# First input block on one DMA queue, the second block held back, the first block's scaling moved ahead, and one idle matmul dropped

## The chip, the cores and the metric

The kernel runs on one core of one Trainium2 chip. The metric is the device time of one execution in microseconds (us); "span" is the profiler's stretch from the first to the last instruction of the program, which is about 1.8 us shorter. Some executions on this chip are slower as a whole. Ratios are computed as the mean time of one kernel's fast runs over the mean of the other's in the same rounds, so they are not quite the ratio of the medians that are quoted beside them.

A timeline line reads: start and duration in us, engine, source line, operation, tile written<-tile read, sizes, count; in brackets the engine's idle time before it and what ended that. PE is TensorE's matmuls, PEld its weight loads, DVE VectorE, ACT ScalarE, POOL GpSimd; SPq and ACTq are DMA issues by SyncE and ScalarE.

## The reference

Four residual layers on x of 2048 rows by 1024 columns in bf16: linear attention, gated MLP, and both again with the same weights.

```python
x = A_x
x = x + _A_ref(_layernorm(x), A_wqkv, A_wo)          # q, k, v = x @ wqkv; linear attention; @ wo
x = x + _B_ref(_layernorm(x), B_W_gate, B_W_up, B_W_down)
x = x + _A_ref(_layernorm(x), A_wqkv, A_wo)
x = x + _B_ref(_layernorm(x), B_W_gate, B_W_up, B_W_down)
```

## The kernel before

x is cut into 16 blocks of 128 rows. The first attention layer normalises block by block, transposes (blocks 0 and 1 on TensorE, later ones by DMA) and projects. A unit is eight matmuls of one block against one weight tile of 1 MB; K has tiles k0 and k1, Q has q0 and q1. The order of the first units is k0 of blocks 0 and 1, k1 of blocks 0 and 1, q0 of blocks 0 and 1, then k0, k1, q0 of block 2 and of block 3, then q1.

```python
def head(self):
    ...
    for _ in range(11):                                  # idle matmuls on zeros
        nc.tensor.matmul(idle, lhsT=zero[:, 0:P], rhs=zero, start=True, stop=True)
    k0, k1, v0, q0, q1 = (ring.place() for _ in range(5))
    self.load_x(0, 0)                                    # SyncE's queue
    self.load_x(0, 1, nc.scalar)                         # ScalarE's queue
    k0(0, H)
    self.load_x(1, None, nc.scalar)
    k0(H, 2 * H)
    self.load_x(2)
    k1()
    self.load_x(3)
    def load():                                          # called in the fourth unit
        for t in range(4, 8):
            self.load_x(t)
        q1()
        ...

def block0():
    stat(0, 0); stat(0, 1); rstd(0)
    stat(1, 0)                                           # block 1's first statistic
    scale(0, 0); scale(0, 1)
    t0 = turn(0, 0); t1 = turn(0, 1)                     # TensorE transposes
    t0("ss")
    stat(1, 1); rstd(1)
    q0(0, 2 * H, self.nc.scalar)                         # q0 on ScalarE's queue
    t1("v")
    k(0, 0, between)          # between(): block 1's scaling and first transposes,
                              # ahead of the last two of the eight matmuls
```

## Time and profile before

| | before |
|---|---|
| time, median of the first 3 runs | 1627.14 us |
| span of the profiled run | 1625.4 us |
| TensorE busy | 1613.2 us, 99% |
| VectorE busy, whole span | 567.7 us, 35% |

TensorE is busy practically all the time, so what counts is when its unbroken work starts and whether it is ever interrupted.

### The profile page before, as it was taken

The page shows a single profiled execution, that of the slowest core. Times are in us where ns is not written, and L with a number is a line of the kernel's source. Part 1 is how long each engine was busy: PE and PEld are TensorE (multiplying, and loading weights), DVE is VectorE, ACT ScalarE, POOL GpSimd, SP SyncE. Part 2 cuts the span into 40 slices and gives each one's busy share as a digit, 9 for nine tenths or more (in the row PEclk, how much of TensorE's full clock was granted, in tenths as well). Part 3 has the DMA queues.
Part 4 walks back from the last instruction along what each step waited for, and adds up shares of the span by engine and source line. Part 5 has one row for each costly group of instructions (what it writes and reads, how often), then busy time and mean ns, then how long its engine had stood idle before and what let it go on. Part 6 is the DMA issues. An engine that isn't in the chain of part 4 may idle for free.

```text
span 1625.4 us, 18607 instructions
## 1 busy us (share of the span) xinstructions
PE 1613.2 (99%) x7605; PEld 739.4 (45%) x7739; DVE 567.7 (35%) x940; ACT 330.4 (20%) x635; POOL 202.1 (12%) x134
## 2 busy tenths in 40 slices
PE   9999999999999999999999999999999999999999
PEld 4444444444444444444444444444444444444444
DVE  8844694113212222222264447932021112111211
ACT  6741212101110210111067312121011101101110
POOL 1449220000000000000023582100000000000000
PEclk9999999999999999999999999999999999999999
DMA  9314547447455545544550157464654455454442
GB/s 269 55 52 66 172 79 203 146 158 215 156 162 195 156 147 165 160 154 139 166 111 1 54 107 240 86 189 145 193 161 152 154 178 155 146 170 150 155 162 71
DMA packets 300358, 235.58 MB, mean 145 GB/s; under 512 B 103408, under 2 KB 296304, under 8 KB 300272
## 3 DMA queue, kind: packets, MB, share of 16 engines
q1 hardware_dynamic: 294192, 228.75, 48.3%
q10 hardware_dynamic: 6080, 5.64, 1.0%
q8 instruction: 60, 0.98, 0.3%
q14 instruction: 26, 0.21, 0.0%
HBM read 201.33 MB, written 8.39 MB: 129 GB/s over the span
## 4 chain that ended last, share of the span: by engine, by line
PE 99%; issue 0%; DMA 0%; DVE 0%; ACT 0%
PE pu L643 24%; PE pg L643 24%; PE acc L667 23%; PE ps L410 14%; PE ps L536 7%; PE ps L445 7%; PE kv L458 0%; PE acc_last L667 0%; DMA x<-in_A_x_dram 0%; PE fold L521 0%; PE tp L262 0%; PE ps L435 0%; ACT L692 0%; DVE xo L684 0%; DVE x L156 0%
## 5 line engine op out<-in xcount | busy, mean ns | idle before, releaser
L643 PEld LDWEIGHTS <-t 128*128 128x128 bf16 x3584 | 350.7, 98 | 422.8
L643 PE MATMUL pu<-xnT,t 128*128 128x512 bf16 x1756 | 420.1, 379 | 2.0
L643 PE MATMUL pg<-xnT,t 128*128 128x512 bf16 x1756 | 419.8, 379 | 1.8
L667 PE MATMUL acc<-t,hT 128*128 128x512 bf16 x1728 | 380.6, 379 | 1.9
L649 DVE TENSOR_TENSOR hT<-pu,rg 128x512 bf16<-128x512 f32 x224 | 154.8, 691 | 571.5 <-PE pu L643 555.0
L648 ACT ACTIVATE rg<-pg 128x512 f32<-128x512 f32 x224 | 133.5, 596 | 736.1 <-PE pg L643 661.7
L667 PEld LDWEIGHTS <-hT 128*128 128x128 bf16 x1820 | 178.1, 98 | 209.0
L410 PE MATMUL ps<-t,xnT 128*128 128x512 bf16 x1024 | 223.4, 379 | 0.2 <-ACT xnT L272 0.2
L410 PEld LDWEIGHTS <-xnT 128*128 128x128 bf16 x1024 | 99.4, 98 | 120.0 <-issue 1.5
L536 PE MATMUL ps<-T,pqT 128*128 128x512 bf16 x500 | 110.2, 379 | 0.6
L147 ACT ACTIVATE rstd<-mv,eps 128x1 f32<-128x1 f32 x64 | 18.8, 294 | 337.7 <-DVE mv L145 337.5
L684 DVE TENSOR_TENSOR xo<-x,acc 128x512 bf16<-128x512 f32 x31 | 21.3, 687 | 170.3 <-PE acc L667 169.5
L489 POOL TENSOR_TENSOR prod<-pq,zrow 128x1024 f32<-128x1024 bf16 x32 | 68.0, 2125 | 85.9 <-DVE den L494 72.4
L140 DVE BATCH_NORM_STATS2 stats<-x 128x6 f32<-128x512 f32 (+1 forms) x120 | 77.9, 671 | 1.2 <-DMA x<-in_A_x_dram 0.4
L536 PEld LDWEIGHTS <-pqT 128*128 128x128 bf16 x512 | 49.9, 98 | 60.4 <-issue 0.5
L425 POOL CAST ksum<-x 128x512 f32<-128x512 bf16 x2 | 1.7, 866 | 605.4 <-DVE x L361 605.4
L681 DVE TENSOR_TENSOR x<-x,acc 128x512 f32<-128x512 f32 x32 | 21.6, 674 | 138.5 <-PE acc L667 137.4
L427 POOL TENSOR_TENSOR ksum<-ksum,slab 128x512 f32<-128x512 f32 x46 | 54.1, 1183 | 80.3 <-DVE slab L361 63.0
L361 DVE SCALAR_TENSOR_TENSOR pq<-ps,e 128x512 bf16<-128x512 f32 x64 | 43.9, 686 | 53.3 <-ACT e L355 51.3
L501 POOL TENSOR_TENSOR pq<-pq,den 128x1024 bf16<-128x1024 bf16 x32 | 61.7, 1936 | 3.1 <-DVE den L496 3.1
L494 DVE TENSOR_REDUCE den<-prod 128x32 f32<-128x1024 f32 x32 | 38.9, 1217 | 54.0 <-POOL prod L489 54.0
L445 PE MATMUL ps<-slab,x 128*128 128x512 bf16 x249 | 55.7, 379 | 0.4
(57 smaller groups left out, 592.5 us busy)
## 6 DMA issues: line engine op xcount, KB each, us to landing
t<-in_B_W_gate_dram SPq DMA_DIRECT2D x56, 1024.0 KB, 7.3
t<-in_B_W_up_dram SPq DMA_DIRECT2D x56, 1024.0 KB, 5.4
t<-in_B_W_down_dram SPq DMA_DIRECT2D x64, 896.0 KB, 5.1
t<-in_A_wqkv_dram SPq DMA_DIRECT2D x10, 1024.0 KB, 5.1
t<-in_A_wo_dram SPq DMA_DIRECT2D x4, 1024.0 KB, 6.7
away<-x SPq DMA_DIRECT2D x8, 512.0 KB, 4.7
x<-away SPq DMA_DIRECT2D x8, 512.0 KB, 8.2
out_dram<-xo ACTq DMA_DIRECT2D x31, 128.0 KB, 2.5
```

What stands on the lines that cost most here:

```text
L140: self.nc.vector.bn_stats(out=stats[:, c, :], in_=src[:, c * fmax:(c + 1) * fmax])
L361: nc.vector.scalar_tensor_tensor(out=out, in0=ps, scalar=0.0, in1=e, op0=ALU.max, op1=ALU.add)
L410: nc.tensor.matmul(by_row(ps), lhsT=self.xnT[l, l_q][:, kt, j * P:(j + 1) * P], rhs=w[:, kt, :].rearrange("p (b i d) -> p i b d", i=R, d=H ...
L427: nc.gpsimd.tensor_tensor(out=ksum[:, cols], in0=ksum[:, cols], in1=pk, op=ALU.add)
L445: nc.tensor.matmul(ps, lhsT=self.xn[l, t][:, d * P:(d + 1) * P], rhs=self.pk[l, t][:, h * NW:(h + 1) * NW], start=(t == 0), stop=(t == sel ...
L489: nc.gpsimd.tensor_tensor(out=prod, in0=pq_of[sc, j], in1=zrow, op=ALU.mult)
L501: nc.gpsimd.tensor_tensor(out=heads(pq), in0=heads(pq), in1=den[:, :].unsqueeze(2).to_broadcast([P, D // HD, HD]), op=ALU.mult)
L536: nc.tensor.matmul(ps, lhsT=pqT[sc][:, g, j * P:(j + 1) * P], rhs=T[g // 2][:, g % 2, n2 * NW:(n2 + 1) * NW], start=(g == 0), stop=(g == G ...
L643: nc.tensor.matmul(ps, lhsT=w[:, kt, fi * P:(fi + 1) * P], rhs=self.xnT[l, q][:, kt, :], start=(kt == 0), stop=(kt == KT - 1))
L648: nc.scalar.activation(out=rg, in_=pg, func=ACT.Relu)
L649: nc.vector.tensor_tensor(out=h[:, fi, :], in0=pu, in1=rg, op=ALU.mult)
L667: nc.tensor.matmul(ps[:, 0:n], lhsT=hT[ft // 4][:, ft % 4, j * P:(j + 1) * P], rhs=wd[:, k, i * n:(i + 1) * n], start=(ft == 0), stop=(ft ...
```

## The change

Its intent: let the first x block land sooner by giving it a queue with nothing beside it, hold the second block's transfer a little (a tiny clear of its first elements on VectorE must come before it), let the first block's scaling not wait for the second block's data, and drop an idle matmul that would then be in the way.

```diff
-        for _ in range(11):
+        for _ in range(10):
...
         self.load_x(0, 0)
-        self.load_x(0, 1, nc.scalar)
+        self.load_x(0, 1)
+
+        nc.vector.memset(self.xb[1][:, 0:2], 0.0)
+        self.load_x(1, None, nc.scalar)
         k0(0, H)
-        self.load_x(1, None, nc.scalar)
         k0(H, 2 * H)
...
             rstd(0)
-            stat(1, 0)
             scale(0, 0)
             scale(0, 1)
+            stat(1, 0)
```

## The prediction

> **What bounds the kernel now.** I read the page first. Its busy line says where the time is: the span is 1625.4 us and TensorE is busy 99% of it. TensorE's granted clock is full in all 40 slices, so no other engine sets the time in the large, and the whole idle time of TensorE is 1625.4 − 1613.2 = 12.2 us.
>
> ```profile
> span 1625.4 us, 18607 instructions
> PE 1613.2 (99%) x7605; PEld 739.4 (45%) x7739; DVE 567.7 (35%) x940; ACT 330.4 (20%) x635; POOL 202.1 (12%) x134
> ```
>
> Then the table of who waited for whom, for TensorE alone, over the whole run. It has three waits, all in the first 8 us. After that TensorE is issued without a break that a releaser explains, so whatever the start gains or loses is carried to the end one for one.
>
> ```profile
> PE idle L222 <- DVE zero L219: 1.3, 1, 1.3
> PE tp L262 <- DVE x L156: 0.6, 1, 0.6
> PE ps L410 <- ACT xnT L272: 0.2, 1, 0.2
> ```
>
> The change touches only this start, so I read the timeline of the first 24 us (start, duration, engine, line, operation, tiles; in brackets the idle time before and who ended it).
>
> ```profile
> 0.74 0.40 SPq L372 DMA_DIRECT2D x<-in_A_x_dram  x1
> 0.76 0.88 ACTq L372 DMA_DIRECT2D x<-in_A_x_dram  x2
> ...
> 1.34 4.67 PE L222 MATMUL idle<-zero 128*128 128x512 bf16 x11 [1.34 <-DVE zero L219]
> ...
> 3.78 1.29 DVE L140 BATCH_NORM_STATS2 st<-x 128x6 f32<-128x512 bf16 x2 [2.49 <-DMA x<-in_A_x_dram]
> ...
> 5.55 0.69 DVE L140 BATCH_NORM_STATS2 st<-x 128x6 f32<-128x512 bf16 x1 [0.24 <-DMA x<-in_A_x_dram]
> 5.67 0.20 ACT L148 ACTIVATE rstd<-rstd 128x1 f32<-128x1 f32 x1
> 6.16 0.72 DVE L156 TENSOR_SCALAR x<-x,mv,rstd 128x512 bf16<-128x512 bf16 x2
> ...
> 7.52 0.21 DVE L145 BATCH_NORM_AGGREGATE mv<-st 128x2 f32<-128x12 f32 x1
> ...
> 8.32 0.73 DVE L156 TENSOR_SCALAR x<-x,mv,rstd 128x512 bf16<-128x512 bf16 x2 [0.31 <-ACT rstd L148]
> 8.79 0.23 PEld L262 LDWEIGHTS <-x 128*128 128x128 bf16 x4 [0.33 <-DVE x L156]
> ...
> 11.32 3.46 PEld L410 LDWEIGHTS <-xnT 128*128 128x128 bf16 x17 [0.21 <-DMA t<-in_A_wqkv_dram]
> ```
>
> The reader is to see three chains that meet at the same instant. **Block 0**: x block 0 lands, two statistics at 3.78, the reciprocal deviation ready at 5.87, scaling at 6.16 (0.29 us late, because the first statistic of block 1 stands ahead of it and waited for its DMA until 5.55), transposes at 6.62, first projection matmul at 7.49. **Block 1**: aggregate at 7.52, scaling at 8.32, transposes at 8.79, its eight matmuls from 9.71 on. **Weights**: the second K weight tile (1 MB) is issued at 2.75 and lands 8.5 us later, at 11.25, and the weight load of the first matmul that uses it starts at 11.32. The matmuls are 0.216 us apart ((20.50 − 0.39)/93 in the unbroken stretch from 9.71), so block 1's eight end at 9.71 + 8 × 0.216 = 11.44: the weights arrive just as TensorE gets there. Block 0's transposes are also close behind the eleven idle matmuls, which end at 6.01.
>
> **What the Trainium skill says.** "DMA: Bandwidth & Descriptors", Queues, rings and completion order: each DMA engine takes the queues with work in turn, packet by packet. The trace agrees: from 2.7 to 3.3 us SyncE's queue had 54.9% of the engines' time and ScalarE's 43.8%; from 3.2 to 3.5, with little left on ScalarE's, SyncE's had 91.4%. So a large transfer on the second queue takes half of the service from the first. "Trainium Kernel Development and Optimization", Key Constraints: queues of several issuers run on the same engines and several issuers save only issue time. The trace agrees: the stretches table has 371 GB/s from 3.0 to 6.6 us and 360 from 6.6 to 11.3, whichever queue is served, and one issue occupies SyncE about 0.45 us (0.74 to 1.19). "TensorE: Matmul & The Clock Gate", Part 1: the HAM clock gate: the array starts at half clock and speeds up after about 3.4 us of sustained activity, in a free-running window. The trace agrees in the pitch: idle matmuls (4.67 − 0.43)/10 = 0.424 us apart, projection matmuls 0.216; the granted-clock column reads 1.00 throughout and does not show it. No page bears on the order of the vector instructions.
>
> **The change, part by part.** I compared the instruction order of both kernels: on VectorE one 128x1 clear is added and one statistic moves; on TensorE one idle matmul goes; on SyncE's queue one transfer comes; on ScalarE's one goes. The rest keeps its order.
>
> *Idle matmul removed:* TensorE is free at 6.01 − 0.43 = 5.58 instead of 6.01. The transposes came at 6.62, so by itself this is worth 0.
>
> *Transfers moved:* SyncE issues the two halves of x block 0 at 0.74 and about 1.19; the weights follow 0.45 us later than before (1.65, 2.15). The clear of block 1 comes after VectorE's clear at 1.01 to 1.28, ends near 1.35, and holds ScalarE's only early transfer to about 1.4 instead of 1.19. Before, the first half shared the engines: the queue table in 0.1 and 0.2 us windows gives SyncE 27 packets before 2.4, 41 from 2.4 to 2.6 (12 for ScalarE) and 88 from 2.6 to 3.1 (100 for ScalarE). A 128 KB half is 128 packets of 1 KB plus, by my reckoning, 16 completions: 144, reached near 3.03, landed at 0.74 + 3.0 = 3.74, 0.7 later. Unshared it has 27 + 53 = 80 by 2.6, and then 32 per 0.1 us (97 in the 0.3 us from 3.2), so it is through at 2.8 and lands near 3.5. The second half follows on the same queue; block 1's transfer joins at about 2.8 (1.4 us after issue, as ScalarE's first packets did), and at 18 packets per 0.1 us its 144 last until 3.6; it lands near 4.3. The first statistic runs 3.55 to 4.2, the second waits to 4.3 and ends at 5.0 (duration 0.69). The aggregate starts at 5.0 instead of 5.10: **0.1 us gained**, not more, as the two halves now arrive in turn.
>
> *Scaling moved ahead:* the reciprocal deviation ends 5.87 − 0.1 = 5.77 and scaling starts at 5.80 instead of 6.16: **0.36 us gained for block 0**. Transposes at 6.26, first matmul near 7.13.
>
> *The price:* both statistics of block 1 now follow the scaling. The pair takes 1.29; the pitch from the first scaling to the next statistic was 6.79 − 6.16 = 0.63. So they run 5.80 + 0.63 = 6.43 to 7.72, and the aggregate starts at 7.75 instead of 7.52: **0.23 us lost for block 1**. Its reciprocal, scaling and transposes follow by the old distances: scaling 8.55, transposes 9.02, its eight matmuls from 9.94 to 11.67.
>
> *What is on the path:* block 0 early does not help, since TensorE takes block 1's transposes in program order, between block 0's sixth and seventh matmul. With block 0's first matmul at 7.13 the sixth would be done near 8.4, and TensorE waits there until 9.02. Before, the sixth was issued 8.58, and one pitch later, 8.79, block 1's transposes were just ready. So the early gain turns into a wait, and the path to the end is block 1's: +0.23. The second K tile has the same bytes ahead of it; the start of the stream loses some 0.1 us by serial issue, and the 1 MB query tile that competes with it on ScalarE's queue is issued 0.23 later (it follows block 1's reciprocal), which gives some of that back. It lands near 11.3, ahead of 11.67, and costs nothing. Sum: 1627.14 + 0.23 = **1627.4 us**.
>
> **The rivals.**
> *Intent fulfilled:* if block 0 lands much earlier (first half before 3.4), block 1's statistics are no later than now, the whole start moves up by up to 0.4 us, but the K weights at 11.25 stop it after about 0.1 to 0.2: 1626.9 to 1627.1. For it: the author removed an idle matmul, as if transposes had come to wait for it. Against: only 27 packets moved before 2.4 with hardly any sharing, so the slow beginning is not the other queue's doing.
> *Weights become the bound:* issued 0.45 us later on SyncE, they could land 0.3 to 0.5 later: 11.6 to 11.75, giving 1627.3 to 1627.5 in place of block 1's wait. For it: arrival is exactly on time now. Against: from 3 us on the engines are full, so the queue, not the issue, sets the landing.
> *The clock:* with ten matmuls the busy stretch is 4.24 instead of 4.67 us, and a window boundary could leave the array slow for the first projections: eight matmuls at 0.21 us extra, about 1.7, partly hidden behind the weights: 1628 to 1628.5. The three runs of before lie within 0.37 us, which speaks against a sensitive point, but only for eleven.
> *Query weights late:* issued at 8.09, landed 6.8 later at 14.89, needed at about 14.9. If the later issue moves them more than 0.23, up to 0.3 more: 1627.7.
>
> **Range and chances.** The middle is 1627.4. Intent fulfilled gives the low end, the two late-weight cases and part of a cold clock the high one, and the three runs' spread of 0.37 us is added: 1626.7 to 1628.2. Two per cent is 32.5 us, while all of TensorE's idle time is 12.2, so faster by 2% is impossible by a change here, and slower would need something not seen: 0.005, 0.99, 0.005.
>
> **What would show it right or wrong.** Right: the first scaling near 5.8 without a statistic ahead of it; the aggregate of block 1 near 7.75; a new TensorE wait of some 0.4 to 0.6 us before block 1's transposes near 9.0; the unbroken stretch of matmuls from about 9.9; no wait for the K weights. Wrong: block 0's statistics starting below 3.4 or above 3.8; a weight wait near 11.5 on TensorE; projection matmuls 0.42 us apart after 7 us; any difference after 30 us that is not the same shift.

## More of the kernel before

The prediction shows the lines; the one to add is from the timeline of the first 24 us: where TensorE's weight loads for the first query unit begin. (Some matmul records are missing from this trace, 7605 of 7739, so small TensorE gaps after 100 us in it are not gaps of the engine.)

```profile
14.94 8.95 PEld L410 LDWEIGHTS <-xnT 128*128 128x128 bf16 x42 [0.16 <-issue]
```

## The result, and the profile after

The changed kernel took 1627.70 us (1627.41 to 1627.76, 6 runs), before 1627.36 (1626.99 to 1627.38, 6 runs): 0.34 us more, ratio 1.0002, 95% interval 0.999 to 1.0015. The interval is some 2 us wide either way, so the ratio alone proves no difference of 0.3 us; that there is a small one is read from the traces below.

The page of the changed kernel begins with (span, then busy time of each engine):

```profile
span 1626.0 us, 18740 instructions
...
PE 1620.9 (100%) x7738; PEld 739.4 (45%) x7738; DVE 567.4 (35%) x941; ACT 330.3 (20%) x635; POOL 202.1 (12%) x134
```

TensorE's busy sum is larger only because this trace has all matmul records. Its table of TensorE's waits over the whole run (us in total, times, longest) has three lines. The longest is that of the idle matmuls, as before; the other two are:

```profile
PE ps L412 <- DMA t<-in_A_wqkv_dram: 0.3, 1, 0.3
PE tp L264 <- DVE x L156: 0.2, 1, 0.2
```

The first is a wait for a weight tile, which before did not have. The timeline of the first 24 us shows how both come about (line numbers are two higher than before):

```profile
3.00 0.69 DVE L140 BATCH_NORM_STATS2 st<-x 128x6 f32<-128x512 bf16 x1 [1.71 <-DMA x<-in_A_x_dram]
...
3.95 0.69 DVE L140 BATCH_NORM_STATS2 st<-x 128x6 f32<-128x512 bf16 x1 [0.26 <-DMA x<-in_A_x_dram]
...
5.49 0.73 DVE L156 TENSOR_SCALAR x<-x,mv,rstd 128x512 bf16<-128x512 bf16 x2 [0.60 <-ACT rstd L148]
...
6.14 1.28 DVE L140 BATCH_NORM_STATS2 st<-x 128x6 f32<-128x512 bf16 x2
...
7.45 0.21 DVE L145 BATCH_NORM_AGGREGATE mv<-st 128x2 f32<-128x12 f32 x1
...
8.72 0.23 PEld L264 LDWEIGHTS <-x 128*128 128x128 bf16 x4 [0.45 <-DVE x L156]
...
11.87 3.35 PEld L412 LDWEIGHTS <-xnT 128*128 128x128 bf16 x17 [0.83 <-DMA t<-in_A_wqkv_dram]
...
15.51 8.51 PEld L412 LDWEIGHTS <-xnT 128*128 128x128 bf16 x40 [0.29 <-issue]
```

The intent was met: block 0's statistics start at 3.00 in place of 3.78 and its scaling at 5.49 in place of 6.16. Block 1 is not later either: its aggregate comes at 7.45 (7.52 before), its transposes at 8.72 (8.79). Then the gain is gone. The second K tile is used from 11.87 on in place of 11.32, and the first query unit starts at 15.51 in place of 14.94, 0.57 us later. The spans differ by 0.6 us, so what follows 15.5 us takes as long as before.

The queue view, for the transfers being issued at 2.7 to 2.8 us before and at 3.2 to 3.25 us after, gives the second K tile (size, us from issue to landing):

```profile
t<-in_A_wqkv_dram SPq DMA_DIRECT2D x1, 1024.0 KB, 8.5
```

```profile
t<-in_A_wqkv_dram SPq DMA_DIRECT2D x1, 1024.0 KB, 8.6
```

Issued at 2.75 and 3.22, it lands at 11.3 and 11.8. The same view at 8.0 to 8.15 us has the query tile, issued by ScalarE at 8.09 before and 8.03 after:

```profile
t<-in_A_wqkv_dram ACTq DMA_DIRECT2D x1, 1024.0 KB, 6.8
```

```profile
t<-in_A_wqkv_dram ACTq DMA_DIRECT2D x1, 1024.0 KB, 7.4
```

It lands at 14.90 and 15.47, 0.04 us ahead of the weight loads of the first query unit. So TensorE is held twice by late weights. From matmul to matmul the trace after has 0.72 us at the second K tile and 0.38 at the query tile, where 0.216 is the usual pitch: 0.50 and 0.17 lost. Less the 0.07 that block 1 is early, that is the 0.6 us between the spans. The query tile is the last to arrive, and by that same 0.04 us its landing alone would have set the same start.

### The profile page after: what moved, and what is told of

It is laid out like the page before. It is cut to its first block, busy times and chain, and to the rows that moved or that the text cites. A ratio compares the mean times of both kernels' runs of the same rounds, so it can differ in the third digit from the quotient of the medians.

```text
span 1626.0 us, 18740 instructions
## 1 busy us (share of the span) xinstructions
PE 1620.9 (100%) x7738; PEld 739.4 (45%) x7738; DVE 567.4 (35%) x941; ACT 330.3 (20%) x635; POOL 202.1 (12%) x134
## 4 chain that ended last, share of the span: by engine, by line
PE 99%; DMA 1%; SPq 0%; DVE 0%; issue 0%
PE pu L645 24%; PE pg L645 24%; PE acc L669 23%; PE ps L412 13%; PE ps L538 7%; PE ps L447 7%; DMA t<-in_A_wqkv_dram 1%; PE kv L460 0%; PE acc_last L669 0%; PE fold L523 0%; SPq L374 0%; SPq L36 0%; PE ps L437 0%; DVE xo L686 0%
```

## The experiments

Twelve runs, each timed in five rounds, and each with one trace. Medians in us; "query start" is where the trace has TensorE's weight loads restart for the first query unit, where they stop at all; "query tile" is when the last of the DMA engines had landed it.

| run | time | before, same rounds | span | query tile | query start |
|---|---|---|---|---|---|
| before (first trace) | 1627.36 | | 1625.4 | 14.90 | 14.94 |
| after (first trace) | 1627.70 | 1627.36 | 1626.0 | 15.47 | 15.51 |
| before_again | 1627.15 | 1627.34 | 1625.5 | 15.01 | no stop |
| after_again | 1627.63 | 1627.34 | 1625.7 | 15.21 | 15.25 |
| order_only | 1627.33 | 1627.34 | 1625.4 | 14.78 | no stop |
| queues_only | 1627.61 | 1627.34 | 1625.8 | 15.35 | 15.39 |
| no_hold | 1628.24 | 1627.40 | 1626.9 | 16.44 | 16.49 |
| hold_only | 1627.40 | 1627.59 | 1625.8 | 15.30 | 15.35 |
| idle11 | 1627.43 | 1627.59 | 1625.5 | 15.03 | 15.08 |
| idle11_again | 1627.84 | 1627.30 | 1626.0 | 15.48 | 15.52 |

In all eight rows with a stop, the query start follows the landing of the query tile by 0.04 to 0.05 us, and span minus query start is 1610.4 to 1610.5 us. **The whole difference between these traces is when the first query unit starts, and the last thing that it waits for is the query tile.** Single executions of one kernel differ by several tenths too; that landings do that as well is seen in the two traces of the changed kernel (15.47 and 15.21) and not shown for executions without a trace.

### The two kernels once more: before_again, after_again

No edit. The question is whether the late weights belong to the change or to one execution.

> The kernel before, unchanged, for a second trace and for the spread. Theory A (the change loses because the second K weight tile lands later; the loss is the systematic lag of its bytes) and theory C (the loss is a hiccup of one or two DMA engines that happened to fall into the changed kernel's profiled run) both expect here a ratio of 1.0000 and an 11.2 to 11.4 us landing of that tile with no TensorE wait for it. If the landing here is 11.6 or later, a late landing is no property of the change, which speaks for C.

> The changed kernel, unchanged. Theory A: the second K tile lands again near 11.8 us, TensorE waits for it again some 0.4 us after block 1's matmuls end at 11.4, and the time is again 0.3 to 0.4 us above before. Theory C: in another run the two late engines are absent, the tile lands near 11.3, TensorE does not wait, and the time of such a run is within 0.1 us of before. Theory B (my prediction: block 1's chain sets the end) has fallen already, since block 1's aggregate came at 7.45, earlier than the 7.52 of before.

Measured: before 1627.15 (ratio 0.9996) and after 1627.63 (median 0.29 above; the ratio is 1.0000 because it goes by means, and one execution of before in these rounds took 1630.23). The second trace of before has no weight wait on TensorE; block 1's matmuls begin at 9.89 there and run on without a stop. The second trace of after has the wait again, smaller (timeline, weight loads):

```profile
11.62 3.35 PEld L412 LDWEIGHTS <-xnT 128*128 128x128 bf16 x17 [0.60 <-DMA t<-in_A_wqkv_dram]
15.25 2.68 PEld L412 LDWEIGHTS <-xnT 128*128 128x128 bf16 x13 [0.28 <-issue]
```

The landing events of the 16 DMA engines, read from the packed trace, tell system from accident. The median engine finished the second K tile at 10.84 and 10.91 before, 10.95 and 11.10 after; the last one at 11.28 and 11.26 before, 11.83 and 11.58 after. So for this tile a small part of the lag is general, and the larger part is the slowest of 16 engines. For the query tile the lag is general: the median engine was done with it at 14.67 and 14.56 before, 15.39 and 15.15 after, there only 0.06 to 0.08 ahead of the last. Theory A holds for the general part, though the tile that sets the start is the query tile; theory C, an accident of one run alone, does not, since the wait recurred, though its size changes.

### The order alone: order_only

```diff
             rstd(0)
-            stat(1, 0)
             scale(0, 0)
             scale(0, 1)
+            stat(1, 0)
```

> The kernel before with only the scaling of block 0 moved ahead of block 1's first statistic; queues and the eleven idle matmuls as before. By the steps of the prediction: scaling of block 0 at 5.90 in place of 6.16, aggregate of block 1 at 7.85 in place of 7.52, its eight matmuls 0.33 us later, end 0.3 us later than before, no wait for weights (landing 11.3). If the second K tile alone sets the time (theory A in its strongest form), the end moves only by what goes beyond its landing, also about 0.3, so this run tests the price of the order, not A. No change in time would mean that the order costs nothing.

Measured: 1627.33 against 1627.34, no change. Block 0's scaling came at 5.54 and block 1's aggregate at 7.51, not 7.85. The distance from first statistic to that aggregate was as reckoned, 7.51 − 3.41 = 4.10 (7.85 − 3.78 = 4.07 expected), but block 0 landed earlier in this run, at 3.4. In the traces of before, before_again, order_only and hold_only, all with the old placement of block 0's halves, the first half landed at 3.76, 3.54, 3.39 and 3.49. In the old order the aggregate follows block 1's landing instead: 5.55 to 7.52 in before. So the order trades one wait for another of about the same length, and no price of 0.33 was seen.

### The queues alone: queues_only

```diff
# the changed kernel, with
-        for _ in range(10):
+        for _ in range(11):
...
             rstd(0)
+            stat(1, 0)
             scale(0, 0)
             scale(0, 1)
-            stat(1, 0)
```

> The changed kernel's queues and hold, but VectorE's old order and eleven idle matmuls. Block 1's x landed at 4.39 us in the changed kernel, so its first statistic fits into the wait for the reciprocal: scaling of block 0 stays at 5.5, aggregate of block 1 comes near 6.85 in place of 7.45, and its matmuls could end near 11.0. Theory A: the second K tile still lands at 11.7 to 11.9, TensorE waits for it 0.6 us or more, and the time is that of the changed kernel (0.3 to 0.4 us above before). Theory B' (VectorE's chain of block 1 sets the end): 0.4 us faster than the changed kernel, so about equal to before or a little under. Theory C: as B' in a run without the late engines.

Measured: 1627.61, as slow as the changed kernel (1627.63 in the same rounds). The timeline has block 1's aggregate half a microsecond earlier than in before and after, and the wait for weights that much longer:

```profile
6.96 0.21 DVE L145 BATCH_NORM_AGGREGATE mv<-st 128x2 f32<-128x12 f32 x1
...
11.78 0.76 PEld L412 LDWEIGHTS <-xnT 128*128 128x128 bf16 x5 [0.95 <-DMA t<-in_A_wqkv_dram]
```

This separates the theories: if VectorE's chain of block 1 set the end, this run had to win 0.4 us. It won nothing, so with the new queues the weights are the bound. Which of the two tiles: the second K tile alone would have allowed a query start near 11.79 + 16 × 0.216 = 15.25, the query tile landed at 15.35.

### What slows the stream: no_hold, hold_only

The stretches view gives the mean rate of all transfers from 1 to 6 us, in its last column. Here before, then after, order_only and hold_only, one fence each:

```profile
1.00:6.00 5.00, 4.66 (x11) 1.49 (x11) 2.23 (x7) 1.51 (x3) 0.29 (x1) 1.00 0.79 271
```

```profile
1.00:6.00 5.00, 4.49 (x11) 1.39 (x12) 2.40 (x9) 1.51 (x3) 0.29 (x1) 1.00 0.78 254
```

```profile
1.00:6.00 5.00, 4.14 (x11) 1.36 (x11) 2.24 (x8) 1.52 (x3) 0.29 (x1) 1.00 0.80 274
```

```profile
1.00:6.00 5.00, 4.66 (x11) 1.49 (x11) 2.31 (x8) 1.51 (x3) 0.29 (x1) 1.00 0.87 273
```

All five traces with block 0's halves on two queues have 266 to 274 GB/s; all nine with both halves on SyncE's queue 238 to 261. 17 GB/s over 5 us are 0.085 MB, which at the 357 GB/s of before from 6 to 11 us is 0.24 us. The deficit arises late in that stretch: in the three microseconds from 3 to 6, before has 383, 386 and 364 GB/s, after 356, 345 and 335, while up to 3 us both had moved some 0.23 MB.

no_hold drops the hold from the changed kernel; hold_only adds only the hold to before.

```diff
# no_hold: the changed kernel, with
-        nc.vector.memset(self.xb[1][:, 0:2], 0.0)
```

> The changed kernel without the clear that holds block 1's transfer, so that ScalarE issues it at 0.76 us as it issued its first transfer before. In three traces with the old queues the stream moved 266 to 274 GB/s from 1 to 6 us, in three with the new ones 244 to 254, some 0.09 MB or 0.25 us less. Theory A1 (the hold starts the second queue late, so the engines see one queue at a time): the rate is back at 265 or more, the second K tile lands near 11.3, the query tile near 15.0, and the time is within 0.1 us of before; x block 0 lands later again, 3.4 to 3.7. Theory A2 (block 0's second half on SyncE's queue pushes the weights back, whatever the second queue does): rate about 250, landings 11.6 to 11.8 and 15.2 to 15.5, the time of the changed kernel.

```diff
# hold_only: the kernel before, with
         self.load_x(0, 1, nc.scalar)
+        nc.vector.memset(self.xb[1][:, 0:2], 0.0)
         k0(0, H)
```

> The kernel before with only the clear that holds block 1's transfer (issue at 1.34 us in place of 1.19); block 0's halves stay one on each queue. By the sum over packets, all four traces with the halves on two queues had moved 1.33 to 1.37 MB by 6 us, all six with both halves on SyncE's queue 1.19 to 1.27. Theory A2 (block 0's second half on SyncE's queue loses the rate): 1.33 MB or more from 1 to 6 us (mean 266 GB/s or more), second K tile near 11.3, time of before within 0.1 us. Theory A1' (the hold loses it): 255 GB/s or less, weights 0.3 us later, time of the changed kernel.

Measured: no_hold got worse, 1628.24 (0.84 above before), rate 238 GB/s, second K tile at 12.90, the last of its engines 1.7 us behind the median one. A1 is refuted: an early second queue did not restore the rate. hold_only has 273 GB/s and 1627.40 (before 1627.59), level within the spread, so the hold is not what costs; of the parts tried, what goes with the slow stream is moving block 0's second half onto SyncE's queue (A2). This move does two things that no run separates: both halves share a queue, and SyncE issues its weights 0.47 us later (the first at 1.66 in place of 1.19, the second K tile at 3.22 in place of 2.75). The second K tile took 8.5 us from issue to landing before and 8.6 after, so the later issue alone is a rival that stands untested; no_hold, with the same issue times and a much later landing, shows only that it isn't all. One engine straggled in hold_only's trace all the same (landing 11.64, median 10.72), and its query start was 15.35: a late engine can come with either arrangement.

What the hold is good for is also seen. The queue view from 1.7 to 2.4 us counts packets in before, after and no_hold (queue 1 is SyncE's, 10 ScalarE's):

```profile
q1 hardware_dynamic: 27, 0.03, 20.5%
q10 hardware_dynamic: 3, 0.00, 1.3%
```

```profile
q1 hardware_dynamic: 125, 0.12, 66.1%
```

```profile
q1 hardware_dynamic: 53, 0.05, 60.2%
q10 hardware_dynamic: 16, 0.03, 25.5%
```

With ScalarE issuing at the same instant as SyncE, SyncE's packets start slowly, though ScalarE's hardly move in that time. With the hold, 125 packets are through, and the first half lands at 2.98. Without it, which is the one edit between these two, 53 are through and it lands at 3.80; before, 27 and 3.76.

### The idle matmul: idle11, idle11_again

```diff
# the changed kernel, with
-        for _ in range(10):
+        for _ in range(11):
```

> The changed kernel with eleven idle matmuls again. All theories: the time of the changed kernel within 0.1 us, since TensorE's first transposes wait for the scaling (5.45 to 5.5 plus 0.47, so 5.95) and the weights for the rest; the eleventh idle matmul ends near 6.0 and can delay the transposes by less than 0.1, which the wait for the second K tile takes up. If the removed matmul had cost the array its full clock, this run would be faster by 0.3 us or more.

> The run idle11 once more, because its median came out 0.16 us under before where the changed kernel came out 0.3 above, in a session whose runs of before themselves spread over 2 us. In its trace the early stream was as slow as in the other runs with both halves on SyncE's queue (254 GB/s), but no engine straggled, and the second K tile landed at 11.35. If the eleventh idle matmul does nothing (all theories), the landing is again 11.3 to 11.8 and the median 0.1 to 0.4 us above before. If it helps, the median is again at or below before.

Measured: 1627.43 (before 1627.59) and 1627.84 (before 1627.30). The two medians straddle before, and the landings in the traced executions go with that: the second K tile at 11.35 and the query tile at 15.03 in the first trace, 11.81 and 15.48 in the second. TensorE's first projection matmul is at 6.97 and 6.70, with ten idle matmuls at 7.04 and 6.79. The eleventh matmul has no effect on the time that these runs show. It can get in the way: in idle11 block 0's scaling began at 5.33 and its transposes only at 6.01, when the last idle matmul ended, 0.68 later in place of 0.47 (5.49 to 5.96 in the changed kernel). The later wait for weights took that up.

### Trying to bring the weights in earlier: q0_ahead, q0_q1_ahead, weights_first, weights_first_old_queues

```diff
# q0_ahead: the changed kernel, with
         k1()
+        q0()
         self.load_x(3)
...
-            q0(0, 2 * H, self.nc.scalar)
```

> The changed kernel with the query tile issued on SyncE's queue behind the second K tile and ahead of x block 3, in place of ScalarE's queue after block 1's reciprocal. In all six traces the span is 1610.4 to 1610.5 us plus the start of the first query matmul, and in the three with the new queues that start comes 0.04 to 0.12 us after... the landing of the query tile (15.21 to 15.47). Theory A: the tile now has 0.25 MB less ahead of it and lands near 14.6; the first query matmul is then bound by the second K tile (11.6 to 11.8 plus 16 matmuls of 0.216) and starts at 15.1 to 15.3: 0.1 to 0.2 us faster than the changed kernel, still not faster than before. If the query tile does not matter: the same as the changed kernel. If x block 3 behind it starves VectorE: slower, with a TensorE wait after 18 us.

Measured: 1628.77 (before 1627.40), ratio 1.0013. The query tile landed at 14.58 and TensorE did not stop at 15 us. The time came back elsewhere. The timelines have x block 3's statistics and TensorE's stop:

```profile
15.33 1.29 DVE L140 BATCH_NORM_STATS2 st<-x 128x6 f32<-128x512 bf16 x2 [2.53 <-DMA x<-in_A_x_dram]
```

```profile
30.19 1.04 PE L412 MATMUL ps<-t,xnT 128*128 128x512 bf16 x4 [1.11 <-DMA t<-in_A_wqkv_dram]
```

Block 3 was late, the transpose that waits for it stands in SyncE's program ahead of the second query tile, and that tile was issued at 21.68 in place of 19.08. From the matmul ahead of the stop to the one after it the trace has 1.49 us in place of the pitch of 0.216, so TensorE lost 1.27 us there. The first query matmul would have been at 11.64 + 16 × 0.216 = 15.10, and 1610.45 + 15.10 + 1.27 = 1626.8, the measured span.

```diff
# q0_q1_ahead: q0_ahead, with
         def load():
+            q1()
             for t in range(4, 8):
                 self.load_x(t)
-            q1()
```

> The run q0_ahead with the second query tile issued ahead of x blocks 4 to 7. In q0_ahead the first query tile came in time (14.58) but TensorE lost 1.27 us at 30.19 us to the second query tile, whose issue had slipped from 19.1 to 21.7 us behind a transpose that waited for x block 3. If that is all, the gap at 30 us is gone and the span is 1610.45 plus the start of the first query matmul, near 15.1: 1625.5 to 1625.6, some 0.2 us under the changed kernel and level with before. If VectorE, which now starts block 3's statistics 2.5 us later and is 99% busy from 30 to 60 us, is the next bound, a TensorE wait for VectorE appears between 30 and 60 us and takes the gain back.

Measured: 1630.68 (before 1627.59), ratio 1.0018, the one run whose 95% interval (1.0005 to 1.003) leaves 1 out. The weight wait at 30 us is gone and VectorE takes its place:

```profile
28.90 1.46 PE L412 MATMUL ps<-t,xnT 128*128 128x512 bf16 x6 [1.72 <-DVE pq L363]
```

VectorE is busy 29.90 of the 30 us from 30 to 60 in before, so the microseconds it idles while waiting for a postponed x block are missed later. From 10 to 60 us it waited 2.2 and 4.1 us for x blocks in q0_q1_ahead, 0.4 in before.

```diff
# weights_first: queues_only, with
         k0(H, 2 * H)
+        k1()
         self.load_x(2)
-        k1()
+        q0()
         self.load_x(3)
...
-            q0(0, 2 * H, self.nc.scalar)
```

> The run queues_only (new queues, old vector order, eleven idle matmuls) with both weight tiles moved ahead of x blocks that are needed later: second K tile before x block 2, query tile before x block 3, both on SyncE's queue. Theory A (weights' landing sets the start of the first query matmul): second K tile lands 0.7 us earlier, near 11.0, the query tile near 14.6, block 1's matmuls end at 11.15 as in queues_only, so the first query matmul starts near 14.6 in place of 15.39 and the span is near 1625.1: 0.7 us under queues_only and 0.3 us under before. Rival (the weights' landing is only a symptom and block 1 or VectorE sets it): no change. Danger: x block 2 lands 3 us later and its transposed block comes too late for the third unit, with a new TensorE wait at 18 us.

> The kernel before with the same two moves of the weight tiles. There block 1's x lands at 5.5 us and its matmuls end at 11.4 to 11.6, so the weights have at most 0.1 us to give. Theory A: the second K tile lands near 10.6 and TensorE is now free of weight waits, but the first query matmul still starts at 11.45 plus 16 times 0.216, 14.9: the time of before within 0.1 us. If it gains 0.3 us or more, the weights were the only bound of before and block 1 was not a second one.

The last run has the same edit on the kernel before. Measured: 1629.05 and 1628.65 (before 1627.40), ratios 1.0009 both. weights_first started its first query unit at 15.17, since a late engine held the query tile to 15.12, and stopped again at 29.81 for the second query tile and at 42.25 and 56.76 for VectorE. In weights_first_old_queues both tiles were early (10.41 and 14.10) and the only later stop is the second query tile's, at 30.24, of 1.52 us (1.74 from matmul to matmul, less the pitch of 0.22); 1626.9 − 1.5 = 1625.4 is before's span. So, as theory A expected, before has nothing to win from weights alone: block 1 holds it at the same instant. None of these four versions beats both kernels.

## Why the prediction was right or wrong

The time was in the range (1627.7 for 1627.4 predicted, +0.34 for +0.23). That the number came so near is luck: block 1's chain was to cost 0.23 and the weights nothing; block 1 came 0.07 early and the weights cost 0.6. Two errors cancelled.

- **TensorE's idle time of 12.2 us**: overstated, since the trace read there lacks 134 matmul records. before_again has them all: 1625.5 − 1620.6 = 4.9 us. The conclusion, that no change here gives 2%, only gets firmer.
- **The idle matmul worth 0**: right for the time; with eleven again, the end did not move.
- **"Transfers moved", 0.1 us gained**: mis-sized. The first half was to land near 3.5 and landed at 2.98, the second near 4.3 and came at 3.93. The working said that the slow beginning, 27 packets before 2.4 us, was not the other queue's doing; with SyncE alone there were 125, and 53 once ScalarE issued beside it again (no_hold).
- **Scaling moved ahead, 0.36 us**: right in mechanism; scaling came at 5.49, a gain of 0.67.
- **"The price", 0.23 us lost for block 1**: failed. The distances were right (6.14 − 5.49 = 0.65 from scaling to statistics, for 0.63; 7.45 − 6.14 = 1.31 to the aggregate, for 1.32), but counted from a scaling 0.31 us earlier than assumed, block 1 was 0.07 us early, not 0.23 late.
- **TensorE waiting for block 1's transposes after its sixth matmul**: mis-sized. The stop was there, but of 0.12 us in place of 0.4 to 0.6: the transposes came at 8.73, and one pitch after the sixth matmul was 8.61. In the first trace TensorE stopped also before its fifth matmul at 8.18, just after the second half of the first K tile landed at 8.13.
- **"The path to the end is block 1's", the second K tile "lands near 11.3, ahead of 11.67, and costs nothing"**: this is the step that failed for the end result. The K tile landed at 11.83 and 11.58 in the two traces, while block 1's matmuls ended near 11.4. The query tile, in the prediction only a rival, landed at 15.47 and 15.21 in place of 14.90 and set the start of the first query unit. The working allowed 0.1 us for serial issue; the stream lost 0.24, and the slowest engine added to it. The argument that full engines make the order of issue harmless was what misled; whether the later issue or the shared queue did it stays open.
- **Rivals**: "Query weights late" (to 1627.7) is what came true, in size too, though not for its reason: the tile was issued no later (8.03 for 8.09) but took 7.4 us in place of 6.8. "Weights become the bound" gave 1627.3 to 1627.5 and was right in kind. "Intent fulfilled" had the right landing and rightly said that the weights would stop it, but not that they would be later. "The clock" did not touch the projections, which were 0.22 us apart from the first on wherever nothing stopped them. But block 0's eight transposes were 0.106 us apart in the first trace after, 0.056 in before. That is not the dropped matmul's doing, since before_again, with eleven, has 0.106 too and after_again, with ten, has 0.056. It cost block 0 some 0.2 us (5.96 to 7.04 in place of 6.62 to 7.49), which the later waits hid.
- **The tests named in advance** worked: statistics starting below 3.4 and a weight wait on TensorE were both listed as signs that the explanation is wrong, and both are in the first trace.

Shown: the new queues, not the order and not the idle matmul, go with later weights; the landing of the query tile gives the start of the first query unit, and that gives the span to 0.1 us. Not shown: whether both halves on one queue or the weights' issue 0.47 us later lowers the rate, by what mechanism, and why single DMA engines lag; the traces do not name the engine of a packet. A difference of 0.3 us is below what the ratios resolve; it rests on the traces and on two medians of the same sign.

## What to carry to other kernels

When data and weights share one full set of DMA engines, landing a small block sooner is worth little if a later weight tile is already arriving just in time: look for the last arrival before TensorE's unbroken stretch (here the query tile), not for the first wait (here the second K tile). Check both halves of such a meeting point before changing one, and look some 15 to 40 us downstream: what is postponed in a queue (here an x block) comes back through queue order and through a busy VectorE. A prediction whose time is right can still rest on the wrong step; naming beforehand what the trace must show is what exposes it.

## What the Trainium skill lacked or had wrong

- "Trainium Kernel Development and Optimization", Key Constraints, says that issuing from several engines only saves issue time. Here it also did harm: a second issuer at the same instant cut the first queue's packets from 1.7 to 2.4 us from 125 (after) to 53 (no_hold). The mean rate from 1 to 6 us, 266 to 274 GB/s with one 128 KB half on the second queue and 238 to 261 without, does not contradict the page, since the saved issue time may be the cause.
- "DMA: Bandwidth & Descriptors", Queues, rings and completion order, says that the engines take the queues they have work for in turn by packet. In the changed kernel, with 1 MB of the first K tile already issued on SyncE's queue, that queue got 15 packets from 3.2 to 3.8 us and ScalarE's 111. Whether SyncE's work was not yet with the engines or they did not take turns is not known, so the page is not shown wrong.
- No page says how far apart the 16 engines of one transfer finish. The last engine was 0.4 us behind the median for the second K tile in before, 0.9 in the changed kernel's first trace and 1.7 in no_hold, and the tile counts as landed only then.
